# Decay attention before two MLPs: one masked product per super-block, keys beside unit matrices, whole token tiles

## The chip, the cores and the metric

One core of a Trainium2 chip runs the whole program. The metric is the device time of one execution in microseconds, the median over the runs. Of the engines, TensorE multiplies matrices, VectorE, ScalarE and GpSimd do elementwise work, and SyncE mostly issues transfers. TensorE writes into PSUM, from where VectorE and ScalarE read.

## The reference

An attention with a decay per head runs in blocks of 64 positions; its output, laid out as 1536 tokens of 512, goes through two MLPs (512 to 2048 to 512) with different activations.

```python
for b in range(nb):                                  # 12 blocks of 64, for 2 batches and 8 heads
    intra = einsum('bhic,bhjc->bhij', qb, kb) * Dmask    # Dmask = lam ** (i - j), 0 above the diagonal
    intra = einsum('bhij,bhjd->bhid', intra, vb)
    inter = einsum('bhid,bhde->bhie', qb * lam_pow, kv_state)
    out[:, :, sl] = intra + inter
    kv_state = lam_block * kv_state + einsum('bhsd,bhse->bhde', kb * rev_pow, vb)
x = out as [1536, 512]
h = x @ w_in;  x = (h * clip(h + 3, 0, 6) / 6) @ w_out     # first MLP
h = x @ w2_in; return maximum(0.01 * h, h) @ w2_out        # second MLP
```

## The kernel before

**Attention.** A super-block `c` (12 of them) holds one block of 64 positions for both batches and all heads. Partitions are split in halves: for batch b, `own[b]` holds its positions and `other[b]` its head dimensions. `scores` makes the 64x64 products of keys and queries, 16 per super-block, on `own[b]`; `mask` multiplies them with `dmask` into one half of the tile `r`, once per batch; `q_decay` multiplies the queries with `lq` into the other half. `attn_out` then contracts all 128 partitions of `r` against `vs`, whose halves are the values and the running state. `state` makes the next state from decayed keys (`k_decay`, tile `kd`) and `vs`, and `state_copy` moves it from PSUM into the next `vs`. `att_x` splits the output in two parts, `xh` and `xl`, the pair of operands with which the MLPs reach float32 precision.

**MLPs.** A step is one slice `f` of 128 hidden units for one tile of 512 tokens (three tiles, `NTT`): `gemm1` (12 matmuls), the gates on ScalarE and VectorE, `gemm2` (12 matmuls into four accumulators). Blocks of 3 to 5 slices (`BLOCKS`) accumulate in PSUM; `collect` adds the sums into SBUF at the end of each block and tile. There are 96 steps; the three of the very first block and tile are split in two halves of 256 tokens. The weights come as 64-bit floats: per half-slice, `low_bits`, `magnitude` and `w_high` on ScalarE and `exponent`, `compose` and `w_low` on VectorE (the first few `w_low` may run on GpSimd) make the two parts `wh` and `wl`.

**Order.** All operations are put into `Order` with an engine or a choice of engines, an estimated time, a due time, what they follow, and what buffers they take and free. `Order.issue` plays the estimates through: when an engine is idle, the ready operation with the earliest due time is issued on it. The result is one fixed instruction order per engine queue; the chip's real times then move it, but not its order. `DUE_C`, `T_FIRST` and `T_MIXED` set the due times, so that before the change attention and the first MLP block are interleaved. Buffers that matter: `q`, `vs` and `raw` have 3, `k` and `r` 2, `w` 8, and the PSUM pools `h` and `a` 2 banks each beside four accumulators `acc0` to `acc3`. `dense` issues matmuls on zeros, whose results nobody reads, beside the first attention products.

Of the kernel before, what the change touches and what calls it, by code (L numbers as in the profile page):

```python
# [18 lines left out]
C = 64  # L19
# [96 lines left out]
def decay_attention_two_mlps(ctx: ExitStack, tc: tile.TileContext, qkk, vv, lam, w1, w2, out):  # L116
# [16 lines left out]
    steps = [(l, b, t, f, cols) for l in range(2) for b in range(len(BLOCKS[l])) for t in range(NTT)  # L133
             for cols in ([(0, TT // 2), (TT // 2, TT)] if l == b == t == 0 else [(0, TT)])
# [3 lines left out]
    for s, (l, b, t, f, _) in enumerate(steps):  # L138
        step_of.setdefault((l, f), s)
        step_of.setdefault((l, b, t), s)  # L140


    due_c = [d for d in DUE_C]
    due1, due2, d = [], [], T_FIRST
    for l, b, t, f, (lo, hi) in steps:
        us = (T_MIXED[t] if l == b == 0 else T_STEP) * (hi - lo) / TT
        due1.append(d)
        due2.append(d + 1.5 * us)
        d += us
# [21 lines left out]
    def warm_up(_):  # L171
        PA["warm"] = new("h", [P, TT], F32)[:, :TT // 2]
        nc.vector.memset(zeros, 0.0)
        dense(N_WARM)

    def consts_a(_):
        TMP["step"], TMP["frst"], TMP["eye_h"] = (new(n, [P, H, C], F32) for n in "uuu")
        eye = TMP["frst"][:, 0, :]
# [5 lines left out]
        nc.vector.tensor_copy(out=TMP["eye_h"], in_=eye.unsqueeze(1).to_broadcast([P, H, C]))  # L184
        nc.vector.memset(TMP["frst"], 0.0)

    def consts_b(_):
        step, frst, eye_h = (TMP[n] for n in ("step", "frst", "eye_h"))
# [4 lines left out]
        nc.vector.tensor_copy(out=frst[:, :, 0:1], in_=lam_b)  # L193

        nc.vector.tensor_tensor_scan(out=flat(dmask), data0=flat(step), data1=flat(eye_h), initial=0.0,
                                     op0=ALU.mult, op1=ALU.add)
        nc.vector.tensor_tensor_scan(out=flat(lq), data0=flat(step), data1=flat(frst), initial=0.0,
                                     op0=ALU.mult, op1=ALU.add)

    def decay_rows(i, b):  # L200
        return lambda e: eng[e].tensor_tensor(
            out=kd[i][other[b], b], in0=TMP["eye_h"][other[b]],
            in1=lq[other[b], :, C - 1:C].to_broadcast([64, H, D]), op=ALU.mult)
# [36 lines left out]
    def k_decay(c, b):  # L240
        return lambda e: eng[e].tensor_tensor(
            out=kd[c % 2][own[b], b], in0=K[c][own[b]],
            in1=dmask[own[b], :, C - 1:C].to_broadcast([64, H, D]), op=ALU.mult)
# [53 lines left out]
    def att_x(c, lo):  # L297
        def fn(_):
            xh, xl = (x.rearrange("p k (c b i) -> p k c b i", c=SPT, b=2)[:, :, c % SPT] for x in X[c // SPT])
            ps = PA["o", c]  # L300
            for i, p in enumerate(ps):
                w = slice(i, i + 1) if len(ps) > 1 else slice(0, 2)
                if lo:
                    nc.vector.tensor_tensor(out=xl[:, :, w], in0=p[:, :, w], in1=xh[:, :, w].bitcast(F32),  # L304
                                            op=ALU.subtract)
                else:
                    nc.scalar.copy(out=xh[:, :, w], in_=p[:, :, w])
# [285 lines left out]
```

## Time and profile before

| | |
|---|---|
| median of 3 runs | 606.07 us (605.94 to 607.43) |
| profiled execution | 606.48 us, its span 604.7 us |
| busy: TensorE, VectorE, ScalarE, GpSimd | 581.4, 413.5, 272.4, 50.3 us |
| mean granted TensorE clock | 0.987 of full speed |
| loads and stores | 49.60 MB |

The span runs from the first instruction to the last; the time holds the little around it too. Busy time of TensorE counts instructions in flight, so a mean length of a matmul there is longer than the pitch at which they follow each other.

### The profile page before, as it was taken

How to read it: one execution, taken by the hardware profiler on the slowest of the kernel's cores; microseconds unless marked ns; L12 is line 12 of the kernel's file. 1: busy time of each engine (PE TensorE's matmuls, PEld its weight loads, DVE VectorE, ACT ScalarE, POOL GpSimd, SP SyncE). 2: the span in 40 equal slices, each digit the busy share in tenths (PEclk: the TensorE clock that was granted, in tenths of full speed). 3: DMA queues.
4: the chain of work that ended last, by engine and by line, in shares of the span. 5: the costliest groups of instructions: out<-in, count | busy, mean ns of one | idle time of the engine just before them, and what ended most of it. 6: DMA issues, size and time to landing. Idle time of an engine off the chain costs nothing.

```text
span 604.7 us, 8843 instructions
## 1 busy us (share of the span) xinstructions
PE 581.4 (96%) x3562; PEld 483.2 (80%) x3562; DVE 413.5 (68%) x654; ACT 272.4 (45%) x460; POOL 50.3 (8%) x43
## 2 busy tenths in 40 slices
PE   7778889999999999999999999999999999999996
PEld 6567867888888888888888888888888888888885
DVE  8999999889649953886448994398437942343333
ACT  2465465867337522754336663476225522222221
POOL 3853560000000000000000000000000000000000
PEclk8978999999999999999999999999999999999999
DMA  8745653334203410322002231034102100000232
GB/s 287 254 133 186 207 172 108 104 109 139 70 2 104 137 38 1 104 73 102 1 1 89 86 118 56 1 105 128 47 1 69 36 1 1 1 0 18 52 70 69
DMA packets 16553, 49.60 MB, mean 82 GB/s; under 512 B 2304, under 2 KB 2304, under 8 KB 16512
## 3 DMA queue, kind: packets, MB, share of 16 engines
q1 hardware_dynamic: 16192, 48.51, 24.8%
q8 instruction: 28, 0.46, 0.3%
q10 hardware_dynamic: 320, 0.52, 0.3%
q14 instruction: 13, 0.11, 0.1%
HBM read 45.88 MB, written 3.15 MB: 81 GB/s over the span
## 4 chain that ended last, share of the span: by engine, by line
PE 85%; DVE 11%; DMA 2%; issue 1%; ACT 1%; SPq 0%; DVEq 0%; ACTq 0%
PE h L427 41%; PE acc L485 35%; PE a L485 7%; DVE t L381 2%; DVE t L383 1%; DVE r L264 1%; DVE t L370 1%; DVE t L373 1%; DVE r L246 1%; PE a L273 1%; DVE xl L304 1%; PE a L292 1%; DMA raw<-w 1%; DMA vs<-vv 1%; DMA lam_sb<-lam 0%
## 5 line engine op out<-in xcount | busy, mean ns | idle before, releaser
L427 PE MATMUL h<-xh,wh 128*128 128x512 f32 (+1 forms) x396 | 153.2, 387 | 1.2 <-DVE xl L304 1.2
L427 PE MATMUL h<-xl,wh 128*128 128x512 f32 (+1 forms) x396 | 152.7, 386 | 0.2 <-DVE xl L304 0.2
L427 PE MATMUL h<-xh,wl 128*128 128x512 f32 (+1 forms) x396 | 152.6, 385 | 0.0
L452 ACT ACTIVATE gh<-u 128x512 fp32r<-128x512 f32 (+1 forms) x99 | 61.2, 619 | 61.1 <-DVE u L446 32.6
L427 PEld LDWEIGHTS h<-xh,wh 128*128 128x128 f32 x396 | 75.5, 191 | 16.2 <-ACT t L364 1.4
L427 PEld LDWEIGHTS h<-xl,wh 128*128 128x128 f32 x396 | 75.5, 191 | 14.7 <-DVE xl L304 0.3
L427 PEld LDWEIGHTS h<-xh,wl 128*128 128x128 f32 x396 | 75.5, 191 | 14.6
L446 DVE TENSOR_TENSOR u<-u,h 128x512 f32<-128x512 f32 x48 | 32.8, 684 | 65.1 <-ACT u L437 65.1
L437 ACT ACTIVATE u<-h 128x512 f32<-128x512 f32 x48 | 28.7, 599 | 105.7 <-PE h L427 105.5
L485 PE MATMUL acc<-gh,wh 128*128 128x512 f32 (+1 forms) x178 | 68.2, 383 | 2.8 <-DVE xl L304 2.8
L485 PE MATMUL acc<-gh,wl 128*128 128x512 f32 (+1 forms) x178 | 67.1, 377 | 0.0
L485 PE MATMUL acc<-gl,wh 128*128 128x512 f32 (+1 forms) x178 | 67.0, 376 | 0.0
L435 ACT ACTIVATE u<-h,three 128x512 f32<-128x512 f32 (+1 forms) x51 | 33.8, 664 | 72.8 <-PE h L427 72.6
L391 ACT CAST wh<-t 128x512 fp32r<-128x512 f32 x64 | 39.5, 621 | 51.6 <-DVE t L383 45.3
L485 PE MATMUL acc<-wh,gh 128*128 128x512 f32 x160 | 62.2, 389 | 0.0
L485 PE MATMUL acc<-wl,gh 128*128 128x512 f32 x160 | 62.2, 389 | 0.0
L485 PE MATMUL acc<-wh,gl 128*128 128x512 f32 x160 | 62.2, 389 | 0.0
L444 DVE SCALAR_TENSOR_TENSOR u<-u,h 128x512 f32<-128x512 f32 (+1 forms) x51 | 33.2, 653 | 26.9 <-ACT u L435 26.7
L496 DVE TENSOR_TENSOR sum<-acc,sum 128x512 f32<-128x512 f32 x60 | 39.3, 683 | 16.1 <-PE acc L485 16.1
L383 DVE CUSTOM_DVE_ANT_0 t<-t,c 128x1024 uint16<-128x1024 uint16 x64 | 48.6, 760 | 2.2
L381 DVE SCALAR_TENSOR_TENSOR t<-raw,t 128x512 uint32<-128x512 uint32 x64 | 47.5, 743 | 1.4
L360 ACT ACTIVATE c<-raw 128x512 uint32<-128x512 uint32 x64 | 42.7, 667 | 9.2 <-DMA raw<-w 9.2
(75 smaller groups left out, 758.9 us busy)
## 6 DMA issues: line engine op xcount, KB each, us to landing
raw<-w SPq DMA_DIRECT2D x64, 512.0 KB, 3.3
q<-qkk SPq DMA_DIRECT2D x12, 512.0 KB, 4.6
vs<-vv SPq DMA_DIRECT2D x24, 128.0 KB, 3.9
k<-qkk SPq DMA_DIRECT2D x11, 256.0 KB, 3.8
out<-sum SPq DMA_DIRECT2D x20, 128.0 KB, 2.3
out<-sum ACTq DMA_DIRECT2D x4, 128.0 KB, 3.2
lam_sb<-lam SPq DMA_DIRECT2D x1, 4.0 KB, 3.0
```

Of the source, the lines that this page charges most:

```text
L360: nc.scalar.activation(out=CV[h][1], in_=RAW[h][:, :, 0], func=AF.Copy, scale=2.0 ** -29)
L381: nc.vector.scalar_tensor_tensor(out=t, in0=RAW[h][:, :, 1], scalar=0xC0000000, in1=t, op0=ALU.bitwise_and, op1=ALU.bitwise_or)
L383: nc.vector.tensor_tensor(out=t, in0=t, in1=c, op=ALU.add)
L391: nc.scalar.copy(out=cut(*h, 0), in_=CV[h][0].bitcast(F32))
L427: nc.tensor.matmul(ps, a[:, 0, ws], x[:, k, :], start=(n == 0), stop=(n == 3 * KC - 1))
L435: nc.scalar.activation(out=U[s], in_=PH[s], func=AF.Relu, bias=three, scale=1.0)
L437: nc.scalar.activation(out=U[s], in_=PH[s], func=AF.Copy, scale=0.01)
L444: nc.vector.scalar_tensor_tensor(out=g, in0=U[s], scalar=6.0, in1=PH[s], op0=ALU.min, op1=ALU.mult)
L446: nc.vector.tensor_tensor(out=g, in0=U[s], in1=PH[s], op=ALU.max)
L452: nc.scalar.activation(out=G[s][0], in_=U[s], func=AF.Copy, scale=1.0 / 6.0 if steps[s][0] == 0 else 1.0)
L485: nc.tensor.matmul(ACC[e], a, x, start=(first and n == 0), stop=(last and n == 2))
L496: nc.vector.tensor_tensor(out=acc, in0=ps, in1=acc, op=ALU.add)
```

## The change

Queries are no longer decayed. The keys of a super-block are copied by ScalarE between unit matrices (`KI`, two buffers inside the sum tiles that the MLPs use later). One product with such a pair of columns as stationary matrix then gives the scores on one half of the partitions and the queries themselves on the other. A single multiplication with the tile `decay`, which holds the mask on one half and the powers for the queries on the other, fills the whole tile `r` (two multiplications for super-block 0). The scores of both batches take a pair of banks (`acc0` or `acc1`), the outputs a bank of `h`.

The due times now put all of the attention in front of the MLPs. The first token tile is no longer split. The MLP accumulators come as two pairs of banks, and a pair is freed when both of its halves are collected. `w_low` runs on VectorE only, and decayed keys of super-blocks from 2 on only on GpSimd. The values of the first two super-blocks are loaded through ScalarE's queue. There are fewer dummy matmuls.

```diff
-DUE_C = [3, 6, 11, 15, 19, 23, 27, 31, 38, 45, 51, 58]
-T_FIRST, T_MIXED, T_STEP, T_COLLECT, HOP = 10.0, (6.5, 9.5, 5.2), 5.2, 2.0, 0.3
+DUE_C = [5.0 + 3.5 * c for c in range(NSC)]
+T_FIRST, T_STEP, T_COLLECT, HOP = 46.0, 5.45, 2.0, 0.3
 LATENCY = {"dma": 1.0, "pe": 0.15, "act": 0.15, "dve": 0.15, "pool": 0.15}
-N_FAST = 4
-N_WARM, T_WARM = 30, 5.4
-N_DENSE = [6, 3, 1, 2] + [0] * 8
+N_WARM, T_WARM = 24, 4.3
+N_DENSE = [4, 2] + [0] * 10
+NK = 2
...
-    od = Order({**sizes, **{f"acc{e}": 1 for e in range(4)}})
+    od = Order({**sizes, "ki": NK, "acc0": 1, "acc1": 1})
...
-    steps = [(l, b, t, f, cols) for l in range(2) for b in range(len(BLOCKS[l])) for t in range(NTT)
-             for cols in ([(0, TT // 2), (TT // 2, TT)] if l == b == t == 0 else [(0, TT)])
+    steps = [(l, b, t, f) for l in range(2) for b in range(len(BLOCKS[l])) for t in range(NTT)
...
-    dmask = const.tile([P, H, C], F32, name="dmask")
-    lq = const.tile([P, H, C], F32, name="lq")
+    eye = const.tile([P, C], F32, name="eye")
+
+    decay = const.tile([P, 2, H, C], F32, name="decay")
     kd = [const.tile([P, 2, H, D], F32, name=f"kd{i}") for i in range(2)]
     SUM = [const.tile([P, KC, TT], F32, name=f"sum{t}") for t in range(NTT)]
+
+
+    KI = [SUM[1 + i].rearrange("p k t -> p (k t)")[:, :(2 * H + 1) * C].rearrange("p (n c) -> p n c", c=C)
+          for i in range(NK)]
...
+        for ki in KI:
+            nc.gpsimd.tensor_copy(out=ki[:, 0::2, :], in_=eye.unsqueeze(1).to_broadcast([P, H + 1, C]))
...
+        for b in range(2):
+            nc.vector.tensor_copy(out=TMP[b][other[b], :, 0:1], in_=lam_b[other[b]])
+            nc.vector.tensor_tensor_scan(out=flat(decay[:, b]), data0=flat(step), data1=flat(TMP[b]), initial=0.0,
+                                         op0=ALU.mult, op1=ALU.add)
...
+                (nc.scalar if c < 2 else nc.sync).dma_start(out=VS[c][own[b], b], in_=vv[c, own[b]])
+                if c == 0:
+                    nc.gpsimd.memset(VS[c][other[b], b], 0.0)
...
-    def q_decay(c, b):
-        return lambda e: eng[e].tensor_tensor(
-            out=R[c][other[b], b], in0=Q[c][other[b], 0], in1=lq[other[b]], op=ALU.mult)
-
-    def s_bank(c):
-        return f"acc{c % 4}" if c <= SPT else "a"
+            in1=decay[own[b], b, :, C - 1:C].to_broadcast([64, H, D]), op=ALU.mult)
 
     def scores(c):
         def fn(_):
-            n = s_bank(c)
-            ps = PA["s", c] = new("a", [P, H, C], F32) if n == "a" else ps_acc.tile([P, H, C], F32, tag=n, name=n)
+
+            n = f"acc{c % 2}"
+            ps = PA["s", c] = ps_acc.tile([P, 2, H, C], F32, tag=n, name=n)
+            ki = KI[c % NK].rearrange("p n c -> p (n c)")
             for h in range(H):
                 for b in range(2):
-                    nc.tensor.matmul(ps[own[b], h, :], Q[c][other[b], 1, h, :], Q[c][other[b], 0, h, :],
+                    lo = (2 * h + 1 - b) * C
+                    nc.tensor.matmul(ps[:, b, h, :], ki[other[b], lo:lo + P], Q[c][other[b], 0, h, :],
                                      start=True, stop=True)
             dense(N_DENSE[c])
         return fn
 
-    def mask(c, b):
-        return lambda e: eng[e].tensor_tensor(
-            out=R[c][own[b], b], in0=PA["s", c][own[b]], in1=dmask[own[b]], op=ALU.mult)
+    def keys(c):
+        return lambda _: nc.scalar.copy(out=KI[c % NK][:, 1::2, :], in_=Q[c][:, 1])
+
+    def mask(c):
+        def fn(_):
+            R[c] = new("r", [P, 2, H, C], F32)
+            for b in ([slice(0, 1), slice(1, 2)] if c == 0 else [slice(0, 2)]):
+                nc.vector.tensor_tensor(out=R[c][:, b], in0=PA["s", c][:, b], in1=decay[:, b], op=ALU.mult)
+        return fn
...
-            ps = PA["o", c] = [new(n, [P, KC, 2, C], F32) if n in "ah" else ps_acc.tile([P, KC, 2, C], F32, tag=n, name=n)
-                               for n in o_banks(c)]
-            k = [slice(0, P)] * 2 if c else own
+            ps = PA["o", c] = new("h", [P, KC, 2, C], F32)
             for b in range(2):
                 for h in range(H):
-                    nc.tensor.matmul(ps[b % len(ps)][own[h % 2], h // 2, b, :], VS[c][k[b], b, h, :],
-                                     R[c][k[b], b, h, :], start=True, stop=True)
+                    nc.tensor.matmul(ps[own[h % 2], h // 2, b, :], VS[c][:, b, h, :], R[c][:, b, h, :],
+                                     start=True, stop=True)
...
-        r = add(("none", 0.0), new_r(c), after=[ld["qk", c]], takes=["r"])
-        side = [("pool", 1.0), ("dve", 0.63)][::-1 if c < N_FAST else 1]
-        ks = [] if last else [add(side, k_decay(c, b),
+        ks = [] if last else [add([("pool", 1.05)] + [("dve", 0.69)] * (c < 2), k_decay(c, b), d,
                                   after=[ld["k", c], op_const, st.get(c - 2)]) for b in range(2)]
-        qs = [add(side, q_decay(c, b), after=[r, op_const])
-              for b in range(2) if c]
-        pe = ("pe", 0.87 + 0.11 * N_DENSE[c])
-        s = add(pe, scores(c), d, after=[ld["qk", c], r, op_warm], takes=[s_bank(c)])
-        ms = [add(("dve", 0.63), mask(c, b), after=[s, r, op_const]) for b in range(2)]
-        add(("none", 0.0), nothing, after=ms, frees=[s_bank(c)])
-        add(("none", 0.0), nothing, after=[s] + qs, frees=["q"])
+        pe = ("pe", 1.15 + 0.11 * N_DENSE[c])
+        kc = add(("act", 0.62), keys(c), d - 0.5, after=[ld["qk", c], op_a], takes=["ki"])
+        s = add(pe, scores(c), d, after=[kc, op_warm], takes=[f"acc{c % 2}"])
+        m = add(("dve", 1.25), mask(c), d + 1.2, after=[s, op_const], takes=["r"], frees=[f"acc{c % 2}"])
+        add(("none", 0.0), nothing, after=[s], frees=["q", "ki"])
...
-                w_ready[h] = add([("dve", 0.6)] + ([("pool", 1.25)] if s < 2 * BLOCKS[0][0] else []), w_low(h), after=[hi],
-                                 frees=["raw", "cv"])
+                w_ready[h] = add(("dve", 0.7), w_low(h), after=[hi], frees=["raw", "cv"])
...
-        return "a" if e < 2 and t % 2 and (l, b) != (0, 0) else f"acc{e}"
+
+        return "a" if e < 2 and steps[s][2] % 2 else f"acc{e // 2}"
...
+                if n == "a":
+                    ACC[e] = new("a", [P, TT], F32)
+                elif e % 2 == 0:
+                    pair = ps_acc.tile([P, 2, TT], F32, tag=n, name=n)
+                    ACC[e], ACC[e + 1] = pair[:, 0], pair[:, 1]
...
+            if pair and e % 2:
+                add(("none", 0.0), nothing, after=sums[-2:], frees=[bank])
```

## Rows read from the trace of the kernel before

**Rows 1.** The page's busy table: busy us, share of the span, instructions.

```profile
PE 581.4 (96%) x3562; PEld 483.2 (80%) x3562; DVE 413.5 (68%) x654; ACT 272.4 (45%) x460; POOL 50.3 (8%) x43
```

**Rows 2.** Busy us (count) of PE, PEld, DVE, ACT, POOL by stretch; granted clock, DMA share, GB/s.

```profile
0.00:50.00 50.00, 36.06 (x533) 30.05 (x534) 46.39 (x56) 20.11 (x36) 30.66 (x29) 0.89 0.70 231
50.00:110.00 60.00, 55.63 (x872) 48.06 (x871) 56.81 (x85) 35.05 (x68) 19.66 (x15) 0.98 0.48 154
110.00:599.70 489.70, 489.67 (x2161) 405.13 (x2159) 309.61 (x513) 217.19 (x358) 0.00 (x0) 1.00 0.18 57
200.00:300.00 100.00, 100.00 (x443) 82.81 (x442) 68.09 (x113) 44.23 (x71) 0.00 (x0) 1.00 0.19 64
```

**Rows 3.** The same view, three short stretches.

```profile
5.00:10.00 5.00, 4.70 (x86) 3.70 (x83) 4.92 (x5) 0.88 (x2) 3.21 (x3) 1.00 1.05 352
10.00:15.00 5.00, 2.91 (x37) 2.55 (x38) 4.89 (x8) 1.16 (x3) 1.49 (x2) 0.67 1.04 379
35.00:40.00 5.00, 5.00 (x50) 4.75 (x49) 4.90 (x6) 3.64 (x8) 2.77 (x2) 0.60 0.51 157
```

**Rows 4.** TensorE in order of time: start us, us, batch, idle before it.

```profile
6.28 1.15 PE L258 MATMUL acc<-q 64*64 64x64 f32 x32
7.36 0.83 PE L169 MATMUL h<-zeros 128*128 128x256 bf16 x6
...
33.68 1.98 PE L292 MATMUL acc<-r,vs 128*64 128x64 f32 x32 [4.15 <-DVE r L264]
...
58.11 1.15 PE L258 MATMUL acc<-q 64*64 64x64 f32 x32
...
59.19 1.15 PE L273 MATMUL a<-vs,kd 128*64 128x64 f32 x32
```

**Rows 5.** Weight loads by line and shape: busy us, mean ns.

```profile
L427 PEld LDWEIGHTS h<-xl,wh 128*128 128x128 f32 x396 | 75.5, 191 | 14.7 <-DVE xl L304 0.3
...
L258 PEld LDWEIGHTS a<-q 64*64 64x64 f32 x224 | 7.1, 134 | 2.7 <-issue 2.3
```

**Rows 6.** VectorE's lines in the first 50 us: busy us, mean ns.

```profile
L373 DVE TENSOR_SCALAR t<-t 128x512 uint32<-128x512 uint32 x6 | 7.1, 1187 | 0.2
L381 DVE SCALAR_TENSOR_TENSOR t<-raw,t 128x512 uint32<-128x512 uint32 x5 | 6.9, 1378 | 0.1
L383 DVE CUSTOM_DVE_ANT_0 t<-t,c 128x1024 uint16<-128x1024 uint16 x5 | 6.8, 1369 | 0.2
L264 DVE TENSOR_TENSOR r<-acc,dmask 64x512 f32<-64x512 f32 x8 | 5.5, 685 | 0.1
L370 DVE TENSOR_SCALAR t<-t 128x512 f32<-128x512 f32 x6 | 4.9, 812 | 0.1
L241 DVE TENSOR_TENSOR kd<-k,dmask 64x512 f32<-64x512 f32 x3 | 2.9, 967 | 0.0
...
L195 DVE TENSOR_TENSOR_SCAN dmask<-u 128x512 f32<-128x512 f32 x1 | 1.2, 1225 | 0.0
```

**Rows 7.** VectorE's lines from 110 to 600 us.

```profile
L383 DVE CUSTOM_DVE_ANT_0 t<-t,c 128x1024 uint16<-128x1024 uint16 x51 | 35.3, 692 | 1.7
...
L373 DVE TENSOR_SCALAR t<-t 128x512 uint32<-128x512 uint32 x51 | 21.8, 427 | 1.7
...
L505 DVE TENSOR_TENSOR xl<-sum,xh 128x1024 fp32r<-128x1024 f32 x6 | 7.3, 1219 | 0.0
```

**Rows 8.** GpSimd's lines in the first 110 us.

```profile
L241 POOL TENSOR_TENSOR kd<-k,dmask 64x512 f32<-64x512 f32 x16 | 19.6, 1228 | 20.3 <-DVE r L264 9.9 <-DMA k<-qkk 4.6 <-DVE t L383 2.3
...
L201 POOL TENSOR_TENSOR kd<-u,lq 64x512 f32<-64x512 f32 x1 | 1.6, 1555 | 5.3 <-DVE lq L197 5.3
```

**Rows 9.** ScalarE's lines in the first 50 us.

```profile
L279 ACT COPY vs<-a 64x512 f32<-64x512 f32 x8 | 4.6, 579 | 4.0 <-PE a L273 3.8
L360 ACT ACTIVATE c<-raw 128x512 uint32<-128x512 uint32 x6 | 4.1, 681 | 7.1 <-DMA raw<-w 7.1
```

**Rows 10.** SyncE's queue in order of time: the first issues of v.

```profile
3.07 2.70 SPq L232 DMA_DIRECT2D vs<-vv  x4
```

More of the change, by code (lines that the diff above doesn't have):

```diff
@@ L137, in decay_attention_two_mlps @@
     step_of = {}
-    for s, (l, b, t, f, _) in enumerate(steps):
+    for s, (l, b, t, f) in enumerate(steps):
         step_of.setdefault((l, f), s)
         step_of.setdefault((l, b, t), s)
[L143 to L149, printed above, removed]
+    due_c = DUE_C
+    due1 = [T_FIRST + T_STEP * s for s in range(NS)]
+    due2 = [d + 1.5 * T_STEP for d in due1]
     own = [slice(0, 64), slice(64, 128)]
@@ L171, in warm_up @@
     def warm_up(_):
-        PA["warm"] = new("h", [P, TT], F32)[:, :TT // 2]
+        PA["warm"] = new("a", [P, TT], F32)[:, :TT // 2]
         nc.vector.memset(zeros, 0.0)
@@ L176, in consts_a @@
     def consts_a(_):
-        TMP["step"], TMP["frst"], TMP["eye_h"] = (new(n, [P, H, C], F32) for n in "uuu")
-        eye = TMP["frst"][:, 0, :]
+        TMP["step"], TMP[0], TMP[1] = (new("u", [P, H, C], F32) for _ in range(3))
         nc.gpsimd.memset(eye, 0.0)
@@ L299, in fn @@
             xh, xl = (x.rearrange("p k (c b i) -> p k c b i", c=SPT, b=2)[:, :, c % SPT] for x in X[c // SPT])
[L300 to L307, printed above, removed]
+            if lo:
+                nc.vector.tensor_tensor(out=xl, in0=PA["o", c], in1=xh.bitcast(F32), op=ALU.subtract)
+            else:
+                nc.scalar.copy(out=xh, in_=PA["o", c])
         return fn
@@ L330, in decay_attention_two_mlps @@
+        m = add(("dve", 1.25), mask(c), d + 1.2, after=[s, op_const], takes=["r"], frees=[f"acc{c % 2}"])
+        add(("none", 0.0), nothing, after=[s], frees=["q", "ki"])
         add(("none", 0.0), nothing, after=ks, frees=["k"] * (not last))
         if not last:
-            st[c] = add(pe, state(c), d + 0.4, after=ks + [s, ld["v", c], ld["v", c + 1]] + copies[c - 1] + (op_rows[c % 2] if c else []),
+            st[c] = add(pe, state(c), d + 1.3, after=ks + [ld["v", c], ld["v", c + 1]] + copies[c - 1] + (op_rows[c % 2] if c else []),
@@ L333, in decay_attention_two_mlps @@
                         takes=["a"])
-            copies[c] = [add(("act", 0.5), state_copy(c, b), after=[st[c]]) for b in range(2)]
+            copies[c] = [add(("act", 0.58), state_copy(c, b), after=[st[c]]) for b in range(2)]
             add(("none", 0.0), nothing, after=copies[c], frees=["a"])
-        banks = o_banks(c)
-        o = add(pe, attn_out(c), d + 0.5, after=qs + ms + [ld["v", c]] + copies[c - 1], takes=banks)
+        o = add(pe, attn_out(c), d + 2.6, after=[m, ld["v", c]] + copies[c - 1], takes=["h"])
@@ L338, in decay_attention_two_mlps @@
         add(("none", 0.0), nothing, after=[o, st.get(c)], frees=["vs", "r"])
         dense_ops += [s, o, st.get(c)] if N_DENSE[c] else []
-        hi = add(("act", 0.57), att_x(c, False), after=[o])
-        x_ready[c] = add(("dve", 0.65), att_x(c, True), after=[hi], frees=banks)
-    att_done = [o]
-    add(("none", 0.0), nothing, after=dense_ops, frees=["h"])
+        hi = add(("act", 0.58), att_x(c, False), d + 4.0, after=[o])
+        x_ready[c] = add(("dve", 0.69), att_x(c, True), d + 5.0, after=[hi], frees=["h"])
@@ L346, in decay_attention_two_mlps @@
+    add(("none", 0.0), nothing, after=dense_ops, frees=["a"])
     RAW, CV, W, w_ready = {}, {}, {}, {}
@@ L418, in fn @@
         def fn(_):
-            l, b, t, f, (lo, hi) = steps[s]
-            xh, xl = (x[:, :, lo:hi] for x in X[t])
+            l, b, t, f = steps[s]
+            xh, xl = X[t]
             wh, wl = W[l, f]
-            ps = PH[s] = new("h", [P, TT], F32)[:, :hi - lo]
+            ps = PH[s] = new("h", [P, TT], F32)
             n = 0
@@ L432, in fn @@
         def fn(_):
[L433 removed]
+            U[s] = new("u", [P, TT], F32)
             if steps[s][0] == 0:
@@ L520, in decay_attention_two_mlps @@
     x2_ready, taken, prev1, prev2 = {}, {}, None, None
[L521 removed]
+    for s, (l, b, t, f) in enumerate(steps):
         first, last = f == starts[l][b], f + 1 == starts[l][b + 1]
[L523 to L525 removed]
+        d = due1[s]
+        xs = x2_ready[t] if l else [x_ready[c] for c in range(t * SPT, (t + 1) * SPT)]
+        g1 = add(("pe", 2.73), gemm1(s), d, after=[w_ready[l, f, 0], prev1] + xs, takes=["h", "G"])
         prev1 = g1
[L527 to L530 removed]
+        ua = add(("act", 0.62), gate_a(s), after=[g1], takes=["u"])
+        gb = add(("dve", 0.67), gate_b(s), after=[ua], frees=["h"])
+        gh = add(("act", 0.62), g_high(s), after=[gb])
+        gl = add(("dve", 0.7), g_low(s), after=[gh], frees=["u"])
         sums = []
@@ L533, in decay_attention_two_mlps @@
             bank = acc_bank(s, e)
-            wait = att_done if first and bank == "a" else []
-            prev2 = add(("pe", 0.65 * part), gemm2(s, e), due2[s], after=[gl, w_ready[l, f, 1], prev2] + wait,
-                        takes=[bank] if first else [], frees=([] if e < 3 else ["G"] + ["w"] * (t == NTT - 1)))
+            pair = bank != "a"
+            prev2 = add(("pe", 0.68), gemm2(s, e), due2[s], after=[gl, w_ready[l, f, 1], prev2],
+                        takes=[bank] if first and not (pair and e % 2) else [],
+                        frees=([] if e < 3 else ["G"] + ["w"] * (t == NTT - 1)))
             if not last:
                 continue
-            c = add(("dve", 0.62) if b else ("act", 0.55), collect(s, e), due2[s] + T_COLLECT, after=[prev2, taken.get((t, e, lo))],
-                    frees=[bank])
+            c = add(("dve", 0.69) if b else ("act", 0.58), collect(s, e), due2[s] + T_COLLECT, after=[prev2, taken.get((t, e))],
+                    frees=[] if pair else [bank])
             sums.append(c)
-            taken[t, e, lo] = c
+            if pair and e % 2:
+                add(("none", 0.0), nothing, after=sums[-2:], frees=[bank])
+            taken[t, e] = c
             if l == 1 and b + 1 == len(BLOCKS[l]):
```

65 lines of the change are left out of this document (19 added, 46 removed).

## Prediction

> **What bounds the kernel now.** I read the page's busy table first [rows 1]: TensorE is busy for 96% of the span, VectorE for 68%. Then the busy times by stretch [rows 2], which split the run in three. From 110 us to 599.7 us TensorE never stops, and a stretch of 100 us inside it holds 443 matmuls: 225.7 ns each, the granted clock at its upper level (2.4 GHz). The two MLPs are 96 whole steps of 24 such matmuls, so one step is 24 x 0.2257 = 5.42 us and all of them 520.1 us. The last 5.0 us hold no matmul at all, only the last sums and the stores. So 604.7 - 520.1 - 5.0 = 79.6 us is what the head costs: all time at the front in which TensorE does something else than MLP work, or nothing. The change can touch little but this number. I call it E.
>
> What is E made of? In the first 110 us TensorE idles (50 - 36.1) + (60 - 55.6) = 18.3 us [rows 2], while VectorE is busy 46.4 of the first 50 us and 56.8 of the next 60: it is the engine that others wait for. The granted clock says the rest: 0.67 from 10 to 15 us and 0.60 from 35 to 40 us, so TensorE spent part of these windows at its lower level, 1.2 GHz [rows 3]. The first window is 2.1 us of its 5 without a matmul; in the second TensorE is busy throughout, but the batch before it had waited 4.15 us for a mask (the entry at 33.68 us in [rows 4]). Low clock comes in or behind a wait.
>
> **The change, on TensorE.** The 35 batches of attention products (12 scores, 11 states, 12 outputs) stay, each 32 matmuls in the trace. Two batches back to back start 1.08 us apart at full clock, 34 ns per matmul; at the lower clock one takes 1.98 [rows 4]. So at today's price 35 x 1.08 = 37.8 us. State and output batches keep their shapes. The scores do not: their stationary matrix grows from 64x64 to 64x128 (a key block and a unit block), and no such matmul is in the trace. Bounds: a weight load lasts 134 ns with 64 columns and 191 ns with 128 [rows 5], so 64 more columns cost 57 ns and 128 columns 114 ns. Today 64-column loads pass at 34 ns, less than their 57 ns, so nearly two go side by side. Nothing extra is the lower end: 1.08 us a batch. No overlap at all is the upper end: 32 x 114 = 3.65 us. I take two side by side, as today: 32 x 57 = 1.82 us, 12 x 0.74 = 8.9 us more in all. Dummy matmuls after the warm-up shrink to 4 x 3 + 2 x 3 = 18; six take 0.83 us [rows 4], so 2.5 us. The first scores start at 6.28 us, when q lands [rows 4]; now ScalarE first copies the keys, 0.58 us by its copy row [rows 9], so some 6.9 us. The sum of TensorE's work outside the MLPs: 6.9 + 37.8 + 8.9 + 2.5 = 56.1 us.
>
> The Trainium skill, "TensorE: Matmul & The Clock Gate", section "Part 3: Packing small matmuls — row/col tiling", has a rule against part of this: a weight load overlaps running matmuls only where the row groups differ. By it the new scores, which alternate between row halves, cost what I take, 56.1 us in all; the state and output batches, which use all rows, would pass at 57 ns and add 23 x 0.74 = 17 us. The trace has both at 34 ns, so here the measurement decides.
>
> Whole token tiles turn six half-wide steps into three whole ones; these are among the 96, so the sum holds them.
>
> **On VectorE.** Removed: the decays of queries that wrote half of r; where VectorE shared the work it cost it time too. The two masks per super-block, 685 ns each [rows 6], become one of 128x1024. Its nearest row is the 128x1024 subtraction at 1.22 us [rows 7]; two of today's would be 1.37 (64 partitions each). I take 1.24, and 12 x 1.24 = 14.9 us. The subtractions of x stay: 12 x 0.69 = 8.2. Constants: both scans at 1.23 [rows 6], and seven fills and copies for which I estimate 2.9 by the 0.43 of a one-source operation on 512 columns [rows 7]: some 5.3 in all. Decays of keys are allowed on VectorE for super-blocks 0 and 1 only; I count two at 0.97 [rows 6]: 1.9. That is 30 us. The first MLP block wants three f, six half-slices of weights. One takes two operations of 0.43 and three of 0.69 = 2.9 us in the steady stage [rows 7], but 0.81 + 1.19 + 1.38 + 1.37 in the first 50 us [rows 6], and w_low's 0.69: 5.4. The masks, which read PSUM, keep 685 ns even then; what is stretched is work on SBUF alone, while GpSimd is busy 30.7 of the 50 us [rows 2] and at rest later. After the change GpSimd still has about 20 decays of keys at 1.23, four constant rows at 1.56 [rows 8], and some 4 us of fills and copies at the front: 35 us, as busy a share as before. So VectorE's sum is 30 + 6 x 5.4 = 62 us, and with the steady price 30 + 6 x 2.9 = 47 us.
>
> **What hides.** ScalarE gets 12 key copies (0.58) and keeps 22 state copies and 12 of x (0.58 each) and three operations of up to 0.68 per half-slice [rows 9]: 46 x 0.58 + 18 x 0.68 = 39 us, below both sums. The loads: q 6.3, k 2.9, v 3.1 and six weight slices 3.1 MB, 15.5 MB; the best rows move 352 and 379 GB/s [rows 3], so 41 to 44 us, and the first q has landed at 6.3: 50 us at most, below TensorE's sum. Four v issues leave SyncE's queue for ScalarE's; they held it 2.70 us in front of the next q [rows 10], and ScalarE has nothing before q lands. If that cover were gone, it would cost these 2.7 us. GpSimd's w_low goes to VectorE, counted above. Accumulators now come in pairs: the first product of a new block waits for two collects instead of one. Between lie 12 matmuls of the next step, 2.7 us, against two collects, which read PSUM like the masks, 0.69 each; VectorE is busy 310 of 490 us there, so I cost it at nothing; uncovered it is 0.7 us at each of seven block ends, 4.8 us. TensorE's queue order is fixed, and output batches now share the two h banks with the MLP's first products; that belongs to the waits below.
>
> **The sum.** E can't be below TensorE's 56.1 unless the wide loads are cheaper, and VectorE, whose queue mixes weights between the masks, asks for up to 62. I take the middle, 59 us. Span: 59 + 520.1 + 5.0 = 584.1 us. The profiled execution took 606.48 us with a span of 604.7, 1.8 more, and lies 0.4 over the median of the runs: 584.1 + 1.8 - 0.4 = 585.5 us. Each time below is E + 526.5 in the same way.
>
> **Rivals.** *The wide loads hide.* For it: today's 34 ns, already below one load. Then TensorE's sum is 47.2 and the transfers' 50 may bind: E 47 to 52, 573.7 to 578.5 us. Chance 0.25.
>
> *The waits stay.* VectorE's weights between the masks make TensorE wait as now: its idle 18.3 us stays on top of 56.1, E 66 to 75. For it: VectorE's 62 us. Against: MLP steps may fill gaps. 592.5 to 601.5 us. Chance 0.10.
>
> *The clock falls.* Dummies now end with super-block 1, and a wait like the 4.15 us ahead of the batch at 33.68 us puts batches at 1.98 [rows 4]. A third of the 35 at that price is 12 x 0.9 = 11 us, E some 70, 596.5 us; all of them 31.5 us, E 87.6 to 91, 614 us and more. Against: in front of each wait stands more TensorE work than now. Chance 0.09, of it 0.02 for a slower kernel. The Trainium skill, same page, section "HAM oscillation — how this bites in real kernels", has this rule: short bursts of matmuls between waits keep falling back to the half clock. The 0.67 and 0.60 of [rows 3] agree.
>
> *Slower: the wide loads do not overlap.* 12 x (3.65 - 1.08) = 31 us on 47.2 makes 78.2 without a single idle microsecond; with 7 us of it, 85.2 and 611.7 us. It decides from E = 79.6: scores of 3.65 us a batch, and 1.4 us of waiting. Against: today's loads do overlap. Chance 0.06, half of it with so little idle that nothing changes (E 77.8 to 81.4).
>
> **How the numbers follow.** My forecast, E 52 to 66 (578.5 to 592.5 us), has 0.50; the rivals 0.25, 0.10, 0.09 and 0.06. 0.3% is 1.8 us, about what this kernel's three runs (605.94 to 607.43) can tell. Faster: 0.50 + 0.25 + 0.10 + 0.07 = 0.92; the same 0.03; slower 0.02 + 0.03 = 0.05. The range runs from E = 47.2 (573) to E = 73 (599), TensorE's 56.1 with nearly all of today's idle time.
>
> **What would show it.** Right: matmuls of the MLPs run without gap from some 60 us on, 443 per 100 us; score batches 1.8 us apart; VectorE over 90% busy before that; weight operations over 1 us beside GpSimd. Wrong: score batches of 1.1 or 3.6 us; a granted clock near 0.5 between 20 and 50 us; a wait of MLP products for weights after the attention; gaps at block ends, where a collect holds a pair of banks.

## The result and the profile after

The changed kernel takes 597.2 us (median of four runs, 595.73 to 598.49) against 606.1 us: a ratio of 0.985, interval 0.982 to 0.988. So it is faster, by 9 us and not by the 20.6 that were forecast. The profiled execution took 595.73 us with a span of 593.9.

The page's busy table of the changed kernel, which answers to [rows 1]: TensorE is still the bound with 582.5 us (581.4 before); VectorE has 24 us less to do and GpSimd 19.

```profile
PE 582.5 (98%) x3466; PEld 486.0 (82%) x3466; DVE 389.5 (66%) x630; ACT 276.8 (47%) x461; POOL 31.1 (5%) x34
```

Busy us (count) of PE, PEld, DVE, ACT, POOL by stretch of the changed kernel, then granted clock, DMA share and GB/s:

```profile
0.00:8.00 8.00, 5.48 (x38) 4.04 (x39) 6.65 (x13) 1.90 (x2) 3.87 (x12) 1.00 0.69 206
8.00:20.00 12.00, 12.00 (x138) 9.88 (x138) 5.14 (x7) 3.04 (x6) 8.24 (x7) 0.57 0.78 236
20.00:30.00 10.00, 10.00 (x248) 9.24 (x246) 4.86 (x7) 6.12 (x11) 4.39 (x5) 1.00 0.77 250
30.00:40.00 10.00, 10.00 (x241) 9.66 (x238) 7.56 (x10) 6.54 (x13) 5.16 (x4) 1.00 0.91 296
40.00:50.00 10.00, 8.61 (x199) 8.00 (x198) 9.35 (x11) 7.42 (x14) 5.95 (x5) 1.00 0.95 280
50.00:60.00 10.00, 9.08 (x221) 8.53 (x220) 9.89 (x13) 7.83 (x15) 3.50 (x3) 1.00 0.90 289
...
70.00:80.00 10.00, 10.00 (x46) 8.29 (x45) 9.79 (x18) 6.91 (x12) 0.00 (x0) 1.00 0.50 155
...
9.00:18.00 9.00, 9.00 (x86) 7.18 (x87) 4.81 (x5) 2.12 (x4) 6.13 (x6) 0.50 0.92 268
```

Two things stand in it. From 8 us on TensorE is hardly ever idle: of the 18.3 us of idle time in the head [rows 2] 5.3 are left, 2.5 of them before 8 us. But from 9 to 18 us its granted clock is 0.50, its lower level of 1.2 GHz, though it is busy in every microsecond. It passes 86 matmuls in those 9 us (ten of them dummies of 256 columns), where later 10 us pass 248.

TensorE of the changed kernel in order of time: start us, us, batch, idle before it.

```profile
1.06 4.70 PE L169 MATMUL a<-zeros 128*128 128x256 bf16 x24 [1.06 <-DVE zeros L173]
7.22 2.62 PE L249 MATMUL acc<-q,sum 64*128 64x64 f32 x32 [1.46 <-ACT sum L255]
9.77 1.04 PE L169 MATMUL a<-zeros 128*128 128x256 bf16 x4
10.74 3.68 PE L249 MATMUL acc<-q,sum 64*128 64x64 f32 x32
...
14.89 1.98 PE L270 MATMUL a<-vs,kd 64*64 64x64 f32 x32
...
19.78 1.15 PE L270 MATMUL a<-vs,kd 128*64 128x64 f32 x32
...
22.59 2.00 PE L249 MATMUL acc<-q,sum 64*128 64x64 f32 x32
24.53 1.15 PE L270 MATMUL a<-vs,kd 128*64 128x64 f32 x32
...
63.40 0.50 PE L408 MATMUL h<-xh,wh 128*128 128x512 f32 x1
...
583.72 0.39 PE L469 MATMUL acc<-wl,gh 128*128 128x512 f32 x1
...
587.35 0.39 PE L469 MATMUL acc<-wh,gl 128*128 128x512 f32 x1
```

The warm-up ends at 5.76 us, and TensorE then rests 1.46 us: the first scores wait for ScalarE's copy of the keys (L255). Behind that rest the second score batch takes 3.68 us; a score batch like it takes 2.00 at 22.59 us. From 22.59 to 24.53 one score batch costs 1.94 us at full clock. The last two rows lie 16 matmuls apart: 3.63 us, or 226.9 ns each.

VectorE of the changed kernel in the first 64 us, by shape: busy us, mean ns. The one mask per super-block takes 1.22 us. Of the operations on weights, two are longer than in the steady stage (1.25 us each, where [rows 7] have 0.69 for the first and the forecast 0.69 for `wl`), one is 0.99 instead of 1.38 in [rows 6], and the two with one source are back at 0.42 and 0.43 from 0.81 and 1.19: 4.3 us for a half-slice, not the 5.4 of the forecast.

```profile
L261 DVE TENSOR_TENSOR r<-acc,decay 128x1024 f32<-128x1024 f32 x11 | 13.4, 1216 | 4.8 <-PE acc L249 4.8
...
L365 DVE CUSTOM_DVE_ANT_0 t<-t,c 128x1024 uint16<-128x1024 uint16 x4 | 5.0, 1246 | 0.1
L363 DVE SCALAR_TENSOR_TENSOR t<-raw,t 128x512 uint32<-128x512 uint32 x5 | 4.9, 987 | 0.0
L377 DVE TENSOR_TENSOR wl<-t,wh 128x512 fp32r<-128x512 f32 x3 | 3.7, 1247 | 0.0
...
L355 DVE TENSOR_SCALAR t<-t 128x512 uint32<-128x512 uint32 x5 | 2.1, 427 | 0.2
```

And the last sums of the changed kernel, on VectorE: it idles 1.99 us before them, until the first accumulators are done. The span ends at 593.9, 6.5 us after the start of the last matmul.

```profile
586.41 2.65 DVE L478 TENSOR_TENSOR sum<-acc,sum 128x512 f32<-128x512 f32 x4 [1.99 <-PE acc L469]
```

Before, it ended 5.4 us after the start of its last matmul:

```profile
599.28 0.39 PE L485 MATMUL acc<-wh,gl 128*128 128x512 f32 x1
```

### The profile page after: what moved, and what is told of

It is laid out like the page before. It is cut to its first block, busy times and chain, and to the rows that moved or that the text cites. A ratio compares the mean times of both kernels' runs of the same rounds, so it can differ in the third digit from the quotient of the medians.

```text
span 593.9 us, 8611 instructions
## 1 busy us (share of the span) xinstructions
PE 582.5 (98%) x3466; PEld 486.0 (82%) x3466; DVE 389.5 (66%) x630; ACT 276.8 (47%) x461; POOL 31.1 (5%) x34
## 2 busy tenths in 40 slices
DMA packets 16551, 49.57 MB, mean 83 GB/s; under 512 B 2304, under 2 KB 2304, under 8 KB 16512
## 4 chain that ended last, share of the span: by engine, by line
PE 93%; DMA 3%; DVE 2%; ACT 1%; SPq 0%; issue 0%; DVEq 0%
PE h L408 44%; PE acc L469 37%; PE a L469 7%; PE acc L249 2%; DMA raw<-w 2%; PE a L270 1%; PE h L283 1%; DMA q<-qkk 1%; PE a L169 1%; DVE r L261 0%; SPq L230 0%; DVE t L365 0%; DVE wl L377 0%; ACT c L342 0%; DVE t L363 0%; DVE xl L292 0%
## 5 line engine op out<-in xcount | busy, mean ns | idle before, releaser
L408 PE MATMUL h<-xh,wh 128*128 128x512 f32 x384 | 149.6, 390 | 0.4 <-DVE u L425 0.4
L408 PE MATMUL h<-xl,wh 128*128 128x512 f32 x384 | 149.4, 389 | 0.0
L408 PE MATMUL h<-xh,wl 128*128 128x512 f32 x384 | 149.4, 389 | 0.0
L433 ACT ACTIVATE gh<-u 128x512 fp32r<-128x512 f32 x96 | 60.7, 632 | 60.6 <-DVE u L427 39.1
L416 ACT ACTIVATE u<-h,three 128x512 f32<-128x512 f32 x48 | 33.1, 689 | 73.8 <-PE h L408 73.6
L469 PE MATMUL acc<-gh,wh 128*128 128x512 f32 x160 | 62.2, 389 | 0.0
L469 PE MATMUL acc<-gl,wh 128*128 128x512 f32 x160 | 62.2, 389 | 0.0
L469 PE MATMUL acc<-gh,wl 128*128 128x512 f32 x160 | 62.2, 389 | 0.0
L377 DVE TENSOR_TENSOR wl<-t,wh 128x512 fp32r<-128x512 f32 x64 | 44.5, 713 | 6.2 <-ACT wh L373 5.6
L443 DVE TENSOR_TENSOR gl<-u,gh 128x512 fp32r<-128x512 f32 x48 | 33.1, 689 | 20.7 <-ACT gh L433 20.6
```

What stands on the lines that cost most here:

```text
L377: return lambda e: eng[e].tensor_tensor(out=cut(*h, 1), in0=CV[h][0].bitcast(F32), in1=cut(*h, 0).bitcast(F32), op=ALU.subtract)
L408: nc.tensor.matmul(ps, a[:, 0, ws], x[:, k, :], start=(n == 0), stop=(n == 3 * KC - 1))
L416: nc.scalar.activation(out=U[s], in_=PH[s], func=AF.Relu, bias=three, scale=1.0)
L433: nc.scalar.activation(out=G[s][0], in_=U[s], func=AF.Copy, scale=1.0 / 6.0 if steps[s][0] == 0 else 1.0)
L443: nc.vector.tensor_tensor(out=gl, in0=U[s], in1=gh.bitcast(F32), op=ALU.subtract)
L469: nc.tensor.matmul(ACC[e], a, x, start=(first and n == 0), stop=(last and n == 2))
```

## The experiments

Theory A: the order is right and TensorE's own work fills the head; what is missing is the clock, lost in the rest of 1.46 us before the first scores. Theory B: the clock is a symptom, and something else (the wide loads, the dummies, pairs of banks, VectorE) takes the time. The expectations give both in numbers.

**More warm-up.** Everything stays, the instruction order too, but the dummies reach to the first scores.

```diff
-N_WARM, T_WARM = 24, 4.3
+N_WARM, T_WARM = 38, 4.3
```

> The changed kernel with 38 instead of 24 warm-up matmuls, the order of everything else untouched. Theory A: in the changed kernel TensorE rests from 5.8 to 7.2 us, the clock falls at about 8.5 us and comes back at 18.5 us, and batches run at half speed in between; that costs 4.6 us. With the rest filled the clock stays up, and the span falls by 4 to 5 us, to about 589.5 us. Rival B: the clock falls because wide score batches with their short rows do not keep it up, whatever stands in front; then the clock is near 0.5 between 9 and 18 us as before and the span changes by less than 1 us.

Measured: 592.3 us (590.41 to 593.66), ratio 0.975, interval 0.972 to 0.979. This is the lowest median of the versions that compute the reference's numbers. Its windows, in the profiled execution (591.25 us):

```profile
8.00:20.00 12.00, 12.00 (x234) 10.19 (x234) 6.24 (x8) 5.24 (x9) 10.51 (x9) 1.00 0.92 291
```

And its TensorE in order of time:

```profile
1.06 6.02 PE L169 MATMUL a<-zeros 128*128 128x256 bf16 x38 [1.06 <-DVE zeros L173]
7.20 2.00 PE L249 MATMUL acc<-q,sum 64*128 64x64 f32 x32
...
15.18 1.15 PE L270 MATMUL a<-vs,kd 128*64 128x64 f32 x32
...
58.95 0.50 PE L408 MATMUL h<-xh,wh 128*128 128x512 f32 x1
```

The first scores start where they did (7.20 us), but now the 12 us pass 234 matmuls instead of 138, and the first product of the MLPs starts at 58.95 instead of 63.40 us. Theory A holds: 4.45 us of head from 14 matmuls that nobody reads. The median is 4.9 us below the first timing of the changed kernel and 3.6 below its second one further down (595.89).

**The order and the lighter work apart.** First the changed kernel with the due times of before, attention and first MLP block interleaved (`due1` and `due2` as before too). In this order the first collected sums overwrite the key buffers, so later super-blocks multiply other numbers; the amount of work is the same.

```diff
-DUE_C = [5.0 + 3.5 * c for c in range(NSC)]
+DUE_C = [3, 6, 11, 15, 19, 23, 27, 31, 38, 45, 51, 58]
```

> The changed kernel with the due times of the kernel before: attention and the first MLP block interleaved again, all else as changed. If attention first carries the gain, this is slower than the changed kernel by several us (600 us and more). If the gain is the lighter VectorE work alone and TensorE is full in any case, it stays within 2 us of the changed kernel's 597 us, since MLP steps done early count as much as late ones.

Measured: 603.39 us, ratio 0.994 (0.991 to 0.996). In the front of its profiled execution the scores start at 6.30 us, 0.34 us behind the same 24 dummies, and the granted clock is 1.00 from 8 to 20 us: there neither the wide products nor the shorter warm-up brought it down without the longer rest.

```profile
6.30 2.00 PE L253 MATMUL acc<-q,sum 64*128 64x64 f32 x32 [0.34 <-issue]
```

In the middle of its head TensorE rests again and the clock is down, as a window of it shows:

```profile
30.00:40.00 10.00, 8.36 (x46) 7.05 (x47) 6.47 (x8) 3.64 (x7) 4.73 (x4) 0.66 0.97 304
```

Then the kernel before with the new due times alone:

```diff
-DUE_C = [3, 6, 11, 15, 19, 23, 27, 31, 38, 45, 51, 58]
-T_FIRST, T_MIXED, T_STEP, T_COLLECT, HOP = 10.0, (6.5, 9.5, 5.2), 5.2, 2.0, 0.3
+DUE_C = [5.0 + 3.5 * c for c in range(NSC)]
+T_FIRST, T_MIXED, T_STEP, T_COLLECT, HOP = 46.0, (5.45, 5.45, 5.45), 5.45, 2.0, 0.3
```

> The kernel before with the due times of the changed one (attention first) and nothing else. If order alone carries the gain: about 597 us. If VectorE stays the engine that the head waits for, with two masks and decays of queries shared with GpSimd: 602 to 610 us, and VectorE busy over 90% until the MLPs run without gap.

Measured: 610.3 us, ratio 1.007 (1.004 to 1.009), slower. Two of its windows: VectorE is full, TensorE waits, and the clock falls to 0.50:

```profile
50.00:60.00 10.00, 5.96 (x121) 5.10 (x117) 9.74 (x12) 6.92 (x13) 4.64 (x4) 1.00 0.68 235
60.00:70.00 10.00, 7.71 (x58) 6.78 (x60) 9.24 (x16) 4.53 (x8) 2.55 (x2) 0.50 0.38 126
```

So all of the change but the order (lighter elementwise work, whole tiles, pairs, fewer dummies; these were not taken apart) brings 0.6%, the order alone loses 0.7%, and both together gain 1.5%: in the new order the old kernel's two masks and decays fill VectorE (9.74 of 10 us).

**Narrow scores back.** Scores of 64x64 again, queries decayed by GpSimd or VectorE, two masks on 64 partitions; order and the rest as after.

```diff
-                    nc.tensor.matmul(ps[:, b, h, :], ki[other[b], lo:lo + P], Q[c][other[b], 0, h, :],
+                    nc.tensor.matmul(ps[own[b], b, h, :], Q[c][other[b], 1, h, :], Q[c][other[b], 0, h, :],
...
+            eng[e].tensor_tensor(out=R[c][other[b], b], in0=Q[c][other[b], 0], in1=decay[other[b], b], op=ALU.mult)
```

> The changed kernel with the one product per head undone: scores from 64x64 key blocks, queries decayed by GpSimd or VectorE as before, masks on half the partitions. Theory A, TensorE bounds the head at 1.93 us a score batch: batches go back to 1.08 us, ten of them 8.5 us less, and up to that comes off the 597 us. Theory B, VectorE and GpSimd take over: 24 decays at 1.0 to 1.6 us on engines that share a port; the head gets no shorter, 597 us or more.

Measured: 596.8 us, ratio 0.984 (0.981 to 0.987), the same as the whole change. The score batches are back at 1.08 us, but a window in the middle of its head reads:

```profile
30.00:40.00 10.00, 6.56 (x192) 6.16 (x192) 9.76 (x11) 4.83 (x9) 8.46 (x7) 1.00 1.01 296
```

VectorE is busy 9.76 of 10 us and TensorE 6.56. Of the waits in the head, 7.0 us are for transfers of q (whose buffers the decays free) and 7.1 for `xl` on VectorE. In these runs the wide product costs TensorE about what it saves the others, and the clock falls in both; this narrow form was not run with 38 dummies, so which is ahead at full clock stays open.

**No dummies between the products,** with 38 at the front.

```diff
-N_DENSE = [4, 2] + [0] * 10
+N_DENSE = [0] * 12
```

> 38 warm-up matmuls, and none of the 18 dummy matmuls behind the products of the first two super-blocks; the order of the rest untouched. If the filled start alone keeps the clock up (the score batches, busy without a pause, do not let it fall), 18 x 0.14 = 2.5 us come off: a span of some 587 us against 589.4 with the dummies. If wide score batches need dummies beside them, the clock falls between 9 and 20 us and the span is 592 us or more.

Measured: a median of 592.32 us, but 590.0 to 596.96: against the first experiment no gain is to be told. The run of 596.96 was the profiled one. TensorE's timeline of it:

```profile
7.33 2.00 PE L249 MATMUL acc<-q,sum 64*128 64x64 f32 x32 [0.67 <-ACT sum L255]
9.65 2.89 PE L249 MATMUL acc<-q,sum 64*128 64x64 f32 x32 [0.32 <-POOL kd L236]
...
53.25 0.91 PE L283 MATMUL h<-r,vs 128*64 128x64 f32 x22 [1.72 <-issue]
```

Two short rests (the 38 dummies took 5.60 us here and 6.02 in the first experiment), and the second score batch is slow again (clock 0.72 from 8 to 20 us); then a rest of 1.72 us at 53 us for which the profile names no other engine, and behind it the clock is 0.75 and 0.74 in the stretches 50 to 60 and 60 to 70 us. What the dummies cost on TensorE (2.5 us by the forecast) was not visible in the median.

**Single banks,** 38 dummies at the front; masks become two of 128x512.

```diff
-    od = Order({**sizes, "ki": NK, "acc0": 1, "acc1": 1})
+    od = Order({**sizes, "ki": NK, **{f"acc{e}": 1 for e in range(4)}})
...
-        return "a" if e < 2 and steps[s][2] % 2 else f"acc{e // 2}"
+        return "a" if e < 2 and steps[s][2] % 2 else f"acc{e}"
```

> 38 warm-up matmuls, and the pairs of banks undone: four single banks, two masks of 128x512 per super-block, each MLP accumulator freed by its own collect. If the pairs cost time only at the very end (the first collect of a pair starts when the second accumulator is done), the time from the start of the last matmul to the end of the span falls from 6.55 to some 5.4 us, and TensorE has no gaps from 70 us on in either. If they also delay block ends, TensorE's last matmul comes earlier too. If two masks instead of one cost the head, the MLPs start later than at 58.95 us.

One run: 597.24 us, with another rest of 2.30 us ("issue") at 35 us and a clock of 0.54 from 40 to 50 us, so its time can't be set beside 592.3. What can be: no gaps at block ends here, and none with pairs (first MLP product to last: 523.96 us here, 523.95 after). The end differs. VectorE's last sums:

```profile
588.03 2.73 DVE L477 TENSOR_TENSOR sum<-acc,sum 128x512 f32<-128x512 f32 x4 [1.31 <-PE acc L468]
```

The last matmul starts at 589.64, and the span ends 5.76 us later, against 6.55 with pairs. Single banks let the sums begin 0.7 us earlier (VectorE idles 1.31 us before them, as in the kernel before, against 1.99). The rest of the end scatters: with pairs it took 6.0 to 6.6 us in the runs with all loads. So pairs cost some 0.7 us, once.

**The changed kernel again,** to see how far its times scatter.

> The changed kernel itself once more, on the same chip as the others, for their comparison: 595.7 to 598.5 us, low clock from 8.5 to 18.5 us.

Measured: 589.9, 594.82, 596.96 and 598.49 us, with mean clocks of 0.999, 0.991, 0.985 and 0.981. The time follows the clock; one of eight runs of the changed kernel in all has a mean clock near 1. The run of 596.96 us was the profiled one. Its dummies took 4.12 us instead of 4.70, the rest is longer, and the clock is 0.50 from 8 to 20 us:

```profile
7.18 3.66 PE L249 MATMUL acc<-q,sum 64*128 64x64 f32 x32 [1.99 <-ACT sum L255]
```

So the program does not fix the rest, nor when the clock falls and returns; why the one run kept it up was not traced.

**Two narrow products for each wide one,** 38 dummies at the front. Each wide product becomes two of 64x64, the scores on one half of the columns and the queries on the other.

```diff
-                    nc.tensor.matmul(ps[:, b, h, :], ki[other[b], lo:lo + P], Q[c][other[b], 0, h, :],
-                                     start=True, stop=True)
+                    for half in own:
+                        nc.tensor.matmul(ps[half, b, h, :], ki[other[b], lo + half.start:lo + half.stop],
+                                         Q[c][other[b], 0, h, :], start=True, stop=True)
```

> 38 warm-up matmuls, and each wide product (key block and unit block, 64x128) as two narrow ones (64x64) on the same moving columns: 64 matmuls a batch in place of 32. The price of a matmul goes with its stationary columns (57 ns for 64 more) and two loads go side by side: by today's pitch of 34 ns a batch takes 64 x 34 = 2.16 us against 1.93, and the span is 2.8 us longer than 589.4. If instead the wide matmul is dear because its load does not overlap at all, the narrow pair is the cheaper one: below 1.9 us a batch.

One run: 594.9 us. Rows of its timeline:

```profile
17.98 1.18 PE L250 MATMUL acc<-q,sum 64*64 64x64 f32 x64
19.10 1.12 PE L271 MATMUL a<-vs,kd 128*64 128x64 f32 x29
...
42.84 0.48 PE L250 MATMUL acc<-q,sum 64*64 64x64 f32 x4 [3.25 <-issue]
43.25 1.97 PE L284 MATMUL h<-r,vs 128*64 128x64 f32 x32
...
62.74 0.50 PE L409 MATMUL h<-xh,wh 128*128 128x512 f32 x1
```

A batch of 64 matmuls takes 1.12 us (17.98 to 19.10), 17.5 ns each: cheaper by 0.8 us than the wide one (1.94). The number is that of the rival in the expectation. What failed is the price behind the other branch, 2.16 us by stationary columns and two loads side by side; the rival's reason, a wide load that does not overlap at all, is not shown by it, since that was worth 3.65 us a batch. But the MLPs start at 62.74, later than with the wide product. Its waits, us in total, times, longest:

```profile
PE acc L250 <- issue: 10.5, 7, 3.2
PE h L284 <- issue: 1.9, 2, 1.4
```

TensorE rests 12.4 us for nothing that the profile names, and the clock falls behind the longest. Timed in a later experiment with the same kernel:

> The kernel with two narrow products once more, now timed in rounds. One look gave 594.9 us with a clock of 0.83 between 40 and 50 us. If that fall is bad luck of the one execution, the median lies near 591 us, at the 592.3 of the wide one or a little under; if its longer waits bring the fall each time, it stays near 595 us.

Measured: 596.06 us, ratio 0.982 (0.980 to 0.985), slower than the wide product with the same warm-up (592.3).

**What those rests are.** Both forms were run with fewer loads: super-blocks from 3 on load no q and from 2 on no k, but use what lies in the earlier ones, so they compute other numbers.

```diff
+            if c >= 3:
+                Q[c] = Q[c - 3]
+                return
...
+            if c >= 2:
+                K[c] = K[c - 2]
+                return
```

> The kernel with two narrow products (38 warm-up matmuls), but super-blocks from 3 on load no q and from 2 on no k: they compute on the tiles of an earlier super-block, so their part of the output is that of other data; values and weights are loaded as before. TensorE's order is the same. If the transfers make TensorE wait in the head, both for q and in the gaps that the trace puts down to nothing but TensorE's own queue (10.5 us in all), these gaps go, and the MLPs start at some 50 us instead of 62.7. If something else sets the pace (VectorE with the weights, ScalarE, GpSimd), the start stays beyond 58 us.

> The same loads left out of the changed kernel with 38 warm-up matmuls and wide products. TensorE bounds its head: its batches sum up to 56 us from the first score on, so the MLPs start at some 56.5 us against 58.95, just the 2.7 us of waits less. If transfers are the bound here too, the start comes clearly earlier than 56 us, which the batches do not allow.

One run each. The narrow form: 590.41 us, MLPs from 57.52 us on, and still rests of 4.9 us before scores and 2.6 us before output batches that the profile puts down to nothing. The wide form: 589.08 us, MLPs from 56.26 us on, and one wait of 0.42 us behind the warm-up. Windows of the wide form:

```profile
30.00:40.00 10.00, 10.00 (x247) 9.66 (x246) 8.93 (x11) 7.22 (x13) 6.34 (x6) 1.00 0.41 124
```

TensorE of the narrow form:

```profile
39.70 0.27 PE L256 MATMUL acc<-q,sum 64*64 64x64 f32 x2 [1.20 <-issue]
...
47.82 0.33 PE L256 MATMUL acc<-q,sum 64*64 64x64 f32 x4 [1.33 <-issue]
...
56.17 0.34 PE L256 MATMUL acc<-q,sum 64*64 64x64 f32 x6 [1.67 <-issue]
```

The rests of the narrow form come 126 or 127 matmuls apart, or two or three times that, whichever batch stands there; 127 matmuls with their weight loads are 254 instructions. That speaks for a supply of instructions that comes in portions, and for transfers that delay it: with all loads the rests were up to 3.25 and 3.70 us in the two profiled runs, with fewer 1.67 at most. This cause was argued, not shown. Shown is that leaving out these loads of q and k shortens the narrow form's rests from 12.4 to 7.5 us and does not end them, and that the wide form without them has nothing but TensorE's own work in its head.

## Why the forecast was too low

**The sum.** The forecast of 585.5 us is 11.7 below the median. By terms: MLP pitch 2.7, head 5.8, end 1.3, and 1.9 by which the median lies higher against the profiled execution than before (1.5 above it, where 0.4 below was taken over): two of the three other runs have a lower mean clock (0.983 and 0.981 against 0.990).

**The step that failed** is the term for the first scores, "some 6.9 us". It moved their start by ScalarE's copy, but did not ask what TensorE does while it waits, although the change also cuts the warm-up by six matmuls; the low clock behind that wait stands in the sum at nothing. With 24 dummies the warm-up ends at 5.76 us, and behind the rest of 1.46 us the clock is at 0.50 from 9 to 18 us: from the start of the first scores to that of the second state batch it takes 12.56 us (7.22 to 19.78), with 38 dummies 7.98 (7.20 to 15.18), so 4.6 us. The rival "The clock falls" had the mechanism, but put it at later waits, at 11 us and 0.09. Its 596.5 us lies near the measured 597.2 by luck: it stands for a head of some 70 us, and the head took 64.8. What it should have weighed is a rest at the very front, where the change itself made one.

That the term came out near (7.2 measured, 6.9 forecast) is luck too. The forecast read 6.28 us as the landing of q, but the kernel before had no rest there: its 30 dummies reach to 6.34 us, and the first q, issued at 1.19 us, took 4.4 us to land, so it was there at 5.6. The first row is of TensorE's timeline, the second of the view of transfers (size, us from issue to landing):

```profile
1.05 5.29 PE L169 MATMUL h<-zeros 128*128 128x256 bf16 x30 [1.05 <-DVE three L183]
...
q<-qkk SPq DMA_DIRECT2D x1, 512.0 KB, 4.4
```

In the changed kernel the same load takes 5.3 us, and ScalarE's copy of the keys starts at 6.51 us:

```profile
q<-qkk SPq DMA_DIRECT2D x1, 512.0 KB, 5.3
...
6.51 0.62 ACT L255 COPY sum<-q 128x512 f32<-128x512 f32 x1 [3.25 <-DMA q<-qkk]
```

The copy alone would have put the scores at some 6.2 us; the other 0.9 us or so are a later q. Two loads of values stand on ScalarE's queue ahead of it, at 0.75 us; the forecast counted their move only as relief for SyncE's queue. The run with narrow scores has them there as well, and its q takes 5.2 us; with the old due times they are issued at 5.58 us, q takes 4.4, and the scores start at 6.30. That they share the transfers with q is the likely cause, but no run changed this alone.

The Trainium skill, "TensorE: Matmul & The Clock Gate", section "HAM oscillation — how this bites in real kernels", tells of waits that put the bursts behind them at the half clock. The trace agrees in this, with a state batch of 1.98 us at 14.89 us, but its rest is 1.46 us, where the waits of the section's example last 3 to 5 us. What no sentence of the prediction had is that a TensorE kept busy by small batches stayed there for 9 us.

**The pitch of the MLP matmuls** was mis-sized: 443 in a window of 100 us counts those cut by its edges. Two starts 16 apart give 226.9 ns, and 2304 x 1.2 ns are 2.7 us. It hid in E: with the right pitch the head before is 599.51 (the last start and one pitch) - 522.8 = 76.7 and after 587.58 - 522.8 = 64.8. The head gained 11.9 us, and the end lost 1.1.

**The rest of the head** went as the sum said: 56.1, first scores +0.3, 12 score batches at 1.94 instead of 1.82 +1.4, low clock +4.6, waits 2.7 (six rests behind 40 us; 2.9 were allowed) make 65.1; measured 64.8. So the price of a wide batch, 1.82, came out near, and the rivals by which wide loads hide (1.08 a batch) or do not overlap (3.65) fell with 1.94. The reason, a price by columns with two loads side by side, is not shown by that: for two narrow products it gave 2.16 us, and 1.12 were measured. *The waits stay* fell too: those 2.7 us, the 1.46 at the front and 1.06 ahead of the warm-up are left of 18.3.

**VectorE** was feared at 62 us and did not set the length of the head: the windows sum to 43.5 us busy in the first 60, 72% and not the 90% that the forecast gave as a sign. It still ends 2.2 of the 2.7 us of waits, all between 45 and 68 us, where it is nearly full (9.35 and 9.89 of 10 us).

```profile
PE h L283 <- DVE r L261: 1.8, 3, 0.8
```

The masks came at 1.22 (1.24 forecast), a half-slice of weights at 4.3 us, between the steady 2.9 and the 5.4 forecast, and some four half-slices lay in the head, not six. The run with narrow scores shows what the wide product spares it: with 64-partition masks and decays VectorE is full.

**Whole token tiles and pairs.** MLP products follow without a gap from 68 us on; pairs cost nothing at block ends, as forecast, but some 0.7 us at the end of the program, where the first collect of the last pair waits for its second accumulator. That term was missing.

## What to carry to other kernels

When an edit puts an operation in front of TensorE's first real work, reach to it with dummy matmuls: a rest of 1.5 us cost 4.5 us here, and it looked like work, since the engine was busy throughout; only the granted clock and the count of matmuls told. A row that starts right behind dummy work does not say when its operand landed; look for the load itself. Take a pitch from two start times, not from a count in a window: half a percent over 2304 matmuls was 2.7 us where the whole gain was 9. An order and the work in it are judged together: either alone was worth 0.6% or less here, and the order alone was a loss.

## What the runs showed of the hardware

- Products of 64x64 on 64 columns pass at 17.5 ns each when four in turn fall on four quarters of the array, at 34 ns when they alternate between two (the narrow scores of [rows 4]), and a 64x128 stationary matrix at 61 ns (1.94 us for 32). The Trainium skill, "TensorE: Matmul & The Clock Gate", section "Part 3: Packing small matmuls — row/col tiling", lets a weight load overlap only where row groups differ; the state and output batches, which use all rows, pass at 34 ns each against loads of 138 and 142 ns in the head of the changed kernel, so here the measurement decides.
- TensorE rested up to 3.7 us for nothing that the profile names in the second profiled run with two narrow products (3.25 us in the first), at most 1.7 us with fewer loads beside it; with the wide product 2.3 us at most, and not at all with fewer loads.
- How long the clock stayed low was not the same in each run of one program: it took 589.9 us at a mean clock of 0.999 and 598.49 at 0.981.
